# Attention with sink rows and a two-layer MLP on one core: the sink rows' copies, their value tile, and seven numbers of the planner

## The chip, the cores and the metric

One Trainium2 chip, one core. The metric is the device time of one launch in microseconds (us), the median of several runs; three runs of the kernel before are shown.

## The reference

```python
B, H, S, D = 4, 8, 768, 64; n_sink, window = 4, 128
scores = (1 / sqrt(D)) * q @ k.T                       # per batch and head
keep = (key < n_sink) | (0 <= query - key < window)    # 4 sink keys and a band of 128
a = softmax(where(keep, scores, -1e9))
x = (a @ v) laid out as [B * S, H * D]                 # 3072 x 512
h = x @ w_in                                           # 512 -> 2048
out = (h - tanh(h)) @ w_out                            # 2048 -> 512
```

All inputs are float32 (the host hands the weights over as 64-bit words, which the kernel decodes).

## The kernel before

The work is cut into 12 chunks of 256 queries (4 batches of 3 chunks), and a chunk into 4 units, u0 to u47, of one pair of heads each. The first three chunks are the first chunks of batches 0, 1 and 2 (units u0 to u11); their attention stands at the head of the program.

A unit's attention: TensorE (PE) makes two tiles of scores (L487 for the first 12 units, L494 later), VectorE (DVE) merges and masks them (L506, L512), ScalarE (ACT) exponentiates (L520, two instructions and two accumulator reads per tile) and scales (L546, four instructions per unit) with the sums that DVE prepares (L540, L541). PE transposes the probabilities (`turn`, L573), ACT and DVE copy them out of PSUM under the band masks (L580, L587). The columns of the four sink keys go another way: GpSimd (POOL) collects them, high and low parts, in the small tile `z` (L551 to L553).

`attend` (L596 to L657) puts two pairs (first three chunks) or four pairs (the rest) together. `sink_rows` transposes `z` on PE into the upper half of the PSUM tile `x` (L604), `sink_copy` copies it to `zr` on ACT (L611), and `values` multiplies: one matmul of 512 columns for each two pairs with the sink values `vsink` (L621), then the band's values (L627). `x_high` (ACT, L639) and `x_low` (DVE, L643) split the result into two parts of a reduced format (fp32r). `x` has one buffer, so the next `sink_rows` waits for `x_low`. In the kernel before `zr` is made twice, by two instructions with a factor of 0 or 1 per row (`odd`), one for each pair of a bank.

`sink_values(b, due)` (L410 to L437) prepares `vsink` for a batch: SP loads `vraw`, ACT copies it into two blocks of 64 rows (`high`, L420), POOL takes the rest and masks it (`low`, L424, L425), DVE adds both under the mask `half` (`total`, L429). It is called for batches 0, 1, 2 in the first three chunks, and four times more later. `sink_half` (L399) makes the masks.

The MLP runs in 96 steps n0 to n95 (a chunk and one of 8 groups of weights each): `first_half` is 24 matmuls of 256 columns (L699), in quarters of 6, `gate` is tanh, difference, high and low part on ACT and DVE (L704 to L715), `second_half` 12 matmuls of 512 columns (L747). `weights(k, g)` decodes group g of w_in (k=0) or w_out (k=1): three DVE passes (L154 to L158), a high part on ACT (L674), a low part on DVE (L679).

Every engine's queue is written in the order of a planner (`Work`, L167 to L228): each piece has an engine, a guessed duration, a due time and the names that it reads and writes; the planner places, engine by engine, the ready piece that is due first. FIRST, EARLY, UNIT, WLEAD, WNEXT, ZL and SV set due times, SLACK a margin ahead of PE's pieces. What counts on the chip is the order that comes out; real waits are semaphores between the engines.

Of the kernel before, what the change touches and what calls it, by code (L numbers as in the profile page):

```python
# [166 lines left out]
class Work:  # L167
# [5 lines left out]
    WAKE = {"PE": 250, "ACT": 170, "DVE": 90, "POOL": 100, "SP": 80}  # L173
    SLACK = 400

# [55 lines left out]
def _banded(tc, qd, kp, vp, vs, masks, w_in, w_out, ident, pts, early, out):  # L231
    nc = tc.nc
    et = mybir.EngineType
    with ExitStack() as ctx:
# [12 lines left out]

        RAW, TWO, CUT, DUO, PB, ZL, TK = 12, 12, 2, 3, 4, 0, 1100

# [6 lines left out]
        NS = len(order)  # L256
        FIRST, EARLY, PACE, LEAD = 50000.0, 5000.0, 7200.0, 16000.0
        UNIT, SECOND, WLEAD, WNEXT = 2200.0, 0.0, 0.0, 2500.0

# [122 lines left out]
        halfi = cpool.tile([P, 1], I32, tag="halfi", name="halfi")  # L382
        vsink = cpool.tile([P, 2, P], F32R, tag="vsink", name="vsink")
        vraw = cpool.tile([P, P], F32, tag="vraw", name="vraw")

        zt = cpool.tile([P, 2, NPAIR, 4, 2, NSK], F32R, tag="z", name="z")

        zr = cpool.tile([P, 2, CH], F32R, tag="zr", name="zr")
        odd = cpool.tile([P, 2], F32, tag="odd", name="odd")
        oddi = cpool.tile([P, 1], I32, tag="oddi", name="oddi")  # L390

        with tc.manual_schedule(engines={et.DVE, et.Pool}):
            mask, above, below, after, rest = masks
            nc.gpsimd.iota(halfi, pattern=[[0, 1]], base=0, channel_multiplier=1)
            nc.gpsimd.iota(oddi, pattern=[[0, 1]], base=0, channel_multiplier=1)
            nc.gpsimd.memset(zt.bitcast(F32), 0.0)
            nc.gpsimd.memset(vsink.bitcast(F32), 0.0)

        def sink_half():  # L399
            for part, bit, pair in ((halfi, 16, half), (oddi, 32, odd)):  # L400
                nc.vector.tensor_scalar(part, part, bit, None, op0=ALU.bitwise_and)
                nc.vector.tensor_copy(pair[:, 0:1], part)
                nc.vector.tensor_scalar(pair[:, 1:2], pair[:, 0:1], 1.0, None, op0=ALU.is_ge)
                nc.vector.tensor_scalar(pair[:, 0:1], pair[:, 0:1], 1.0, None, op0=ALU.is_lt)

        work.add("DVE", 1300, 4000, sink_half, (), ["half"])
        work.add("DVE", 1000, 500, rest, (), ["mask"])
        count = [0]

        def sink_values(b, due):  # L410
            slot = "vraw"

            def load():
                nc.sync.dma_start(vraw, vs[32 * b : 32 * b + 32].rearrange("r (p c) -> p r c", c=P))

            rows = [(slice(64 * i, 64 * i + 64), i) for i in range(2)]

            def high():
                for r, i in rows:
                    nc.scalar.copy(vsink[r, i, :], vraw[r])  # L420

            def low():
                for r, i in rows:
                    nc.gpsimd.tensor_tensor(vraw[r], vraw[r], vsink[r, i, :].bitcast(F32), op=ALU.subtract)  # L424
                nc.gpsimd.tensor_scalar(vraw, vraw, half[:, 1:2], 1.0, op0=ALU.mult, op1=ALU.mult)  # L425

            def total():
                for r, i in rows:
                    nc.vector.scalar_tensor_tensor(  # L429
                        vsink[r, i, :], vsink[r, i, :].bitcast(F32), half[r, 0:1], vraw[r],  # L430
                        op0=ALU.mult, op1=ALU.add,
                    )
# [163 lines left out]
        def attend(cc, p0, pairs):  # L596
# [456 lines left out]
```

## Time and profile before

| | us |
|---|---|
| median of 3 runs | 693.4 (692.64 to 693.81) |
| the profiled execution | 693.47 |
| its span, first to last instruction | 691.7 |
| PE busy in it | 677.0 (98%) |
| DVE, ACT, POOL busy | 427.4, 367.8, 54.5 |

The profile is of one execution. The span leaves out some 1.8 us around the instructions. A busy PE is not PE at its peak: matmuls overlap, and their ends are modelled, so that the step from one start to the next tells more than a duration.

### The profile page before, as it was taken

What the parts mean: (1) busy time and instruction counts of PE and PEld (TensorE: products, weight loads), DVE (VectorE), ACT (ScalarE), POOL (GpSimd) and SP (SyncE); (2) the same over time, 40 slices, a digit from 0 to 9 for tenths busy, and PEclk for the clock granted to TensorE, in tenths of its full rate; (3) what the DMA queues carried; (4) which work ended last, traced back from release to release, by engine and by line L of the source; (5) the groups of instructions that cost most, each with busy time, mean ns of one, the idle gap of its engine ahead of it and who ended that gap; (6) DMA issues with size and microseconds to landing.
All of it is one profiled execution on the core that took longest, in us unless ns stands there. A gap on an engine that the chain in (4) does not pass through costs nothing.

```text
span 691.7 us, 12427 instructions
## 1 busy us (share of the span) xinstructions
PE 677.0 (98%) x4604; PEld 599.7 (87%) x4604; DVE 427.4 (62%) x1084; ACT 367.8 (53%) x1001; POOL 54.5 (8%) x202
## 2 busy tenths in 40 slices
PE   6989999999999999999999999999999999999996
PEld 5668999999988989889988988998898888998985
DVE  6889999946856556646655665565554755663221
ACT  4996433346754555446545645555555545644222
POOL 6331100000000010000001000001000000000000
PEclk9999999999999999999999999999999999999999
DMA  6879801011231032012113202012112101100001
GB/s 177 266 239 383 320 1 32 0 58 59 57 108 33 28 103 59 28 30 91 51 28 108 54 27 90 28 54 80 37 36 80 55 28 59 58 1 1 31 1 35
DMA packets 31713, 52.14 MB, mean 75 GB/s; under 512 B 3228, under 2 KB 21020, under 8 KB 31644
## 3 DMA queue, kind: packets, MB, share of 16 engines
q1 hardware_dynamic: 31340, 50.93, 23.0%
q8 instruction: 38, 0.62, 0.4%
q10 hardware_dynamic: 304, 0.33, 0.2%
q14 instruction: 31, 0.25, 0.1%
HBM read 44.96 MB, written 6.29 MB: 74 GB/s over the span
## 4 chain that ended last, share of the span: by engine, by line
PE 92%; ACT 4%; DVE 1%; SPq 1%; DMA 1%; issue 0%; DVEq 0%
PE h L699 39%; PE o L747 39%; PE s L494 5%; PE x L627 5%; PE t L573 3%; ACT p L546 1%; ACT p L520 1%; PE x L621 1%; DMA pt<-kp 1%; DMA qk<-kp 0%; DVE pt L587 0%; DVE p L512 0%; ACT pt L580 0%; PE x L604 0%; ACT zr L611 0%
## 5 line engine op out<-in xcount | busy, mean ns | idle before, releaser
L699 PE MATMUL h<-xh,w 128*128 128x256 f32 x1536 | 285.4, 280 | 0.0
L699 PEld LDWEIGHTS h<-xh,w 128*128 128x128 f32 x1536 | 240.3, 188 | 2.2 <-issue 0.5
L699 PE MATMUL h<-xl,w 128*128 128x256 f32 x768 | 214.7, 279 | 0.6 <-DVE xl L643 0.6
L747 PE MATMUL o<-w,gh 128*128 128x512 f32 x768 | 199.5, 400 | 0.0
L747 PEld LDWEIGHTS o<-w,gh 128*128 128x128 f32 x768 | 137.5, 188 | 27.3 <-issue 0.3
L699 PEld LDWEIGHTS h<-xl,w 128*128 128x128 f32 x768 | 144.2, 188 | 2.3 <-DVE xl L643 1.0
L747 PE MATMUL o<-w,gl 128*128 128x512 f32 x384 | 106.1, 397 | 0.0
L520 ACT ACTIVATE p<-p,st 128x132 f32<-128x132 f32 x192 | 76.1, 399 | 53.9 <-DVE st L512 53.0
L715 DVE TENSOR_TENSOR gl<-h,gh 128x512 fp32r<-128x512 f32 x96 | 66.2, 689 | 50.6 <-ACT gh L711 50.4
L704 ACT ACTIVATE graw<-h 128x512 f32<-128x512 f32 x96 | 57.0, 594 | 69.8 <-PE h L699 69.7
L707 DVE TENSOR_TENSOR h<-h,graw 128x512 f32<-128x512 f32 x96 | 66.5, 692 | 44.5 <-ACT graw L704 43.9
L711 ACT CAST gh<-h 128x512 fp32r<-128x512 f32 x96 | 55.6, 579 | 58.7 <-DVE h L707 58.7
L747 PEld LDWEIGHTS o<-w,gl 128*128 128x128 f32 x384 | 71.1, 188 | 17.3 <-issue 1.0
L506 DVE COPY_PREDICATED s<-above,s 128x256 f32<-128x256 uint32 x80 | 34.1, 426 | 83.0 <-PE s L494 80.8
L546 ACT ACTIVATE p<-p,st 128x132 f32<-128x132 f32 x192 | 61.8, 395 | 4.5 <-DVE st L541 4.1
L512 DVE CUSTOM_DVE_ANT_0 p<-s,mask 128x132 f32<-128x132 f32 x192 | 48.9, 293 | 6.5 <-PE s L487 0.2
L551 POOL CAST z<-p 128x16 fp32r<-128x16 f32 x48 | 11.8, 246 | 501.6 <-ACT p L546 492.6
L461 ACT CAST q<-qraw 128x512 fp32r<-128x512 f32 x36 | 22.4, 622 | 53.7 <-PE s L494 50.2
L494 PEld LDWEIGHTS s<-ks,q 128*128 128x128 f32 x288 | 42.8, 188 | 4.8 <-issue 0.2
L494 PE MATMUL s<-ks,q 128*128 128x260 f32 x288 | 46.6, 284 | 0.0
L643 DVE TENSOR_TENSOR xl<-x,xh 128x512 fp32r<-128x512 f32 x24 | 16.5, 690 | 43.8 <-ACT xh L639 43.8
L456 DVE TENSOR_TENSOR ks<-kraw,ks 64x392 fp32r<-64x392 f32 x72 | 40.4, 561 | 3.1 <-ACT ks L451 0.9
(82 smaller groups left out, 574.6 us busy)
## 6 DMA issues: line engine op xcount, KB each, us to landing
qraw<-qd SPq DMA_DIRECT2D x36, 256.0 KB, 2.7
wraw<-w_in SPq DMA_DIRECT2D x16, 512.0 KB, 8.9
wraw<-w_out SPq DMA_DIRECT2D x16, 512.0 KB, 9.3
kraw<-kp SPq DMA_DIRECT2D x37, 196.0 KB, 2.7
v<-vp SPq DMA_DIRECT2D x27, 256.0 KB, 2.9
out<-ob SPq DMA_DIRECT2D x24, 256.0 KB, 2.5
qk<-kp SPq DMA_DIRECT2D x8, 196.0 KB, 4.6
qk<-qd SPq DMA_DIRECT2D x16, 64.0 KB, 4.7
```

What stands on the lines that cost most here:

```text
L456: nc.vector.tensor_tensor(k[o, h, :], t[r, :], k[r, h, :].bitcast(F32), op=ALU.subtract)
L494: nc.tensor.matmul(ps[h][:, :WIN], lhsT=q[:, h, t * P : (t + 1) * P], rhs=rhs, start=i == 0, stop=i == 1,)
L512: nc.vector.tensor_tensor_reduce(out=pr[u][:, j, :], in0=ps[h][:, P:WIN], in1=mask[:, kind, :], scale=-0.125, scalar=BIG, op0=ALU.add, op1 ...
L520: nc.scalar.activation(e, e, AF.Exp, bias=st[u][:, j : j + 1], scale=-1.0, accum_out=st[u][:, 4 + j : 5 + j],)
L546: nc.scalar.activation(pr[u][:, j, :], pr[u][:, j, :], AF.Copy, scale=s[:, 8 + j : 9 + j])
L627: nc.tensor.matmul(xps[key][(p - p0) // 2][h * 64 : h * 64 + 64, p % 2, a:z], lhsT=vt[cc, i][:, hd : hd + D], rhs=rhs, start=False, stop=p ...
L699: nc.tensor.matmul(hps[n][:, f, :], lhsT=w, rhs=x, start=r == 0, stop=r == 11)
L704: nc.scalar.activation(gr[n], hps[n], AF.Tanh)
L707: nc.vector.tensor_tensor(hps[n], hps[n], gr[n], op=ALU.subtract)
L711: nc.scalar.copy(gh[n], hps[n])
L715: nc.vector.tensor_tensor(gl[n], hps[n], gh[n].bitcast(F32), op=ALU.subtract)
L747: nc.tensor.matmul(ops[cc, t], lhsT=(gh, gh, gl)[i][n][:, f, t * P : (t + 1) * P], rhs=wt[1, g][:, (0, 1, 0)[i], f, :], start=first and no ...
```

## The change

The changed kernel copies the transposed sink rows once and unmasked into `zr` (one ACT instruction of 256 columns instead of two). `vsink` becomes a tile with a block of 128 columns for each of the four pairs, zero outside the pair's 32 rows, and `values` multiplies once per pair (256 columns) instead of once per two pairs (512 columns). `high` writes four blocks of 32 rows on ACT with the factor `half` (+1 or -1) from a per-row operand, `total` adds four blocks on DVE; POOL's `low` is gone, and the four instructions of `sink_half` that made `odd`. Seven numbers of the planner move, one (SV) is new, and the guessed durations of `high`, `total`, `sink_copy` and `sink_half` are adapted.

```diff
-    SLACK = 400
+    SLACK = 350
...
-        RAW, TWO, CUT, DUO, PB, ZL, TK = 12, 12, 2, 3, 4, 0, 1100
+        RAW, TWO, CUT, DUO, PB, ZL, TK, SV = 12, 12, 2, 3, 4, 4000, 1100, 14000
...
-        FIRST, EARLY, PACE, LEAD = 50000.0, 5000.0, 7200.0, 16000.0
-        UNIT, SECOND, WLEAD, WNEXT = 2200.0, 0.0, 0.0, 2500.0
+        FIRST, EARLY, PACE, LEAD = 45000.0, 4600.0, 7200.0, 16000.0
+        UNIT, SECOND, WLEAD, WNEXT = 2400.0, 0.0, 6000.0, 3500.0
...
-        vsink = cpool.tile([P, 2, P], F32R, tag="vsink", name="vsink")
+        vsink = cpool.tile([P, NPAIR, P], F32R, tag="vsink", name="vsink")
...
-        zr = cpool.tile([P, 2, CH], F32R, tag="zr", name="zr")
+        zr = cpool.tile([P, CH], F32R, tag="zr", name="zr")
...
         def sink_half():
-            for part, bit, pair in ((halfi, 16, half), (oddi, 32, odd)):
-                nc.vector.tensor_scalar(part, part, bit, None, op0=ALU.bitwise_and)
-                nc.vector.tensor_copy(pair[:, 0:1], part)
-                nc.vector.tensor_scalar(pair[:, 1:2], pair[:, 0:1], 1.0, None, op0=ALU.is_ge)
-                nc.vector.tensor_scalar(pair[:, 0:1], pair[:, 0:1], 1.0, None, op0=ALU.is_lt)
+            nc.vector.tensor_scalar(halfi, halfi, 16, None, op0=ALU.bitwise_and)
+            nc.vector.tensor_copy(half[:, 0:1], halfi)
+            nc.vector.tensor_scalar(half[:, 1:2], half[:, 0:1], 1.0, None, op0=ALU.is_ge)
+            nc.vector.tensor_scalar(half[:, 0:1], half[:, 1:2], -2.0, 1.0, op0=ALU.mult, op1=ALU.add)
...
-            rows = [(slice(64 * i, 64 * i + 64), i) for i in range(2)]
+            rows = [(slice(32 * p, 32 * p + 32), p) for p in range(NPAIR)]
             def high():
-                for r, i in rows:
-                    nc.scalar.copy(vsink[r, i, :], vraw[r])
-            def low():
-                for r, i in rows:
-                    nc.gpsimd.tensor_tensor(vraw[r], vraw[r], vsink[r, i, :].bitcast(F32), op=ALU.subtract)
-                nc.gpsimd.tensor_scalar(vraw, vraw, half[:, 1:2], 1.0, op0=ALU.mult, op1=ALU.mult)
+                for r, p in rows:
+                    nc.scalar.activation(vsink[r, p, :], vraw[r], AF.Copy, scale=half[r, 0:1])
             def total():
-                for r, i in rows:
+                for r, p in rows:
                     nc.vector.scalar_tensor_tensor(
-                        vsink[r, i, :], vsink[r, i, :].bitcast(F32), half[r, 0:1], vraw[r],
-                        op0=ALU.mult, op1=ALU.add,
+                        vsink[r, p, :], vraw[r], half[r, 1:2], vsink[r, p, :].bitcast(F32), op0=ALU.mult, op1=ALU.add,
                     )
...
-            def sink_copy(m):
-                nc.scalar.activation(zr[:, m, :], xps[key][0][:, 1, :], AF.Copy, scale=odd[:, m : m + 1])
+            def sink_copy():
+                nc.scalar.copy(zr, xps[key][0][:, 1, :])
...
-                for i in banks:
-                    nc.tensor.matmul(xps[key][i], lhsT=vsink[:, p0 // 2 + i], rhs=zr, start=True, stop=False)
+                for p in range(p0, p0 + pairs):
+                    nc.tensor.matmul(
+                        xps[key][(p - p0) // 2][:, p % 2], lhsT=vsink[:, p], rhs=zr, start=p % 2 == 0, stop=False,
+                    )
...
-        sink_values(0, 10000)
+        sink_values(0, SV)
```

Three places of the order. The first is PE around the end of the second chunk's attention: `x1_2` is the result of its second half, `h0` and `h1` the first layer of steps n0 and n1, `t8` and `t9` the transposes of units u8 and u9, `x2_0` the `sink_rows` of the third chunk. Before:

```order
L573 MATMUL t7_732<-ident_58,p7_566 128x128 x4
...
L487 MATMUL s11_1_760<-qk10_324 128x260 x2
L573 MATMUL t8_772<-ident_58,p8_623 128x128 x4
L621 MATMUL x1_2_746<-zr_250,vsink_247 128x512
...
L699 MATMUL h0_810<-xh0_514,w0_0_741 128x256
L573 MATMUL t9_835<-ident_58,p9_673 128x128 x4
...
L604 MATMUL x2_0_861<-ident_58,z_249 128x128 x2
L699 MATMUL h1_865<-xh1_717,w0_0_741 128x256
```

In the changed kernel (its lines stand some 10 lower here):

```order
L689 MATMUL h0_732<-xh0_516,w0_0_595 128x256
...
L563 MATMUL t7_742<-ident_58,p7_565 128x128 x4
...
L477 MATMUL s11_1_762<-qk10_321 128x260 x2
L563 MATMUL t8_781<-ident_58,p8_622 128x128 x4
L610 MATMUL x1_2_758<-zr_250,vsink_247 128x256 x2
...
L689 MATMUL h0_732<-xh0_516,w0_0_595 128x256
L689 MATMUL h1_843<-xh1_723,w0_0_595 128x256
...
L563 MATMUL t9_856<-ident_58,p9_671 128x128 x4
L594 MATMUL x2_0_871<-ident_58,z_249 128x128 x2
L689 MATMUL h1_843<-xh1_723,w0_0_595 128x256
```

The first quarter of n0 (six matmuls, of which the first is shown) now stands ahead of u7's transposes, and the other three quarters with the first of n1 ahead of u9's (`t9`); before, two quarters of n0 stood there. The third chunk's `sink_rows` (`x2_0`) now stands ahead of n1's second quarter.

The second place is ACT around `sink_copy` of the second chunk's second half (`zr` from `x1_2`), as far as its `x_high` (`xh1` from `x1_2`); `p9`, `p10`, `p11` are the probabilities of u9 to u11. Before:

```order
L611 ACTIVATE zr_250<-x1_2_746,odd_251 128x256 x2
L520 ACTIVATE p10_737,st10_738<-p10_737,st10_738 128x132 x2
L546 ACTIVATE p9_673<-p9_673,st9_674 128x132 x4
L520 ACTIVATE p10_737,st10_738<-p10_737,st10_738 128x132 x2
L520 ACTIVATE p11_768,st11_769<-p11_768,st11_769 128x132 x2
L420 CAST vsink_247<-vraw_248 64x128 x2
L580 COPY pt_60<-t8_772 128x2x128
L639 CAST xh1_717<-x1_2_746 128x512
```

Changed:

```order
L510 ACTIVATE p10_726,st10_727<-p10_726,st10_727 128x132 x2
...
L510 ACTIVATE p10_726,st10_727<-p10_726,st10_727 128x132 x2
L600 CAST zr_250<-x1_2_758 128x256
L536 ACTIVATE p9_671<-p9_671,st9_672 128x132 x4
L536 ACTIVATE p10_726<-p10_726,st10_727 128x132 x4
L510 ACTIVATE p11_773,st11_774<-p11_773,st11_774 128x132 x2
L417 ACTIVATE vsink_247<-vraw_248,half_245 32x128 x4
L570 COPY pt_60<-t8_781 128x2x128
L630 CAST xh1_723<-x1_2_758 128x512
```

The two tiles of u10's exponents, which stood behind, now stand ahead of the copy, and u10's scaling (`p10`, four instructions) has moved in ahead of `xh1`.

The third place is DVE from u8's masks (`t8`) to u9's (`t9`): `xl1` is `x_low` of the same half chunk, `vsink` the `total` of batch 2. Before:

```order
L587 TENSOR_TENSOR pt_60<-t8_772,below_87 128x2x128
L587 TENSOR_TENSOR pt_60<-t8_772,after_88 128x2x128
L643 TENSOR_TENSOR xl1_718<-x1_2_746,xh1_717 128x512
L429 SCALAR_TENSOR_TENSOR vsink_247<-vsink_247,half_245,vraw_248 64x128 x2
L587 TENSOR_TENSOR pt_60<-t9_835,below_87 128x2x128
```

Changed:

```order
L577 TENSOR_TENSOR pt_60<-t8_781,below_87 128x2x128
L577 TENSOR_TENSOR pt_60<-t8_781,after_88 128x2x128
L158 SCALAR_TENSOR_TENSOR pt_60<-wraw1_0_439,pt_60 128x1024
L421 SCALAR_TENSOR_TENSOR vsink_247<-vraw_248,half_245,vsink_247 32x128 x4
L634 TENSOR_TENSOR xl1_724<-x1_2_758,xh1_723 128x512
L577 TENSOR_TENSOR pt_60<-t9_856,below_87 128x2x128
```

`x_low` stood ahead of `total` and stands behind it now, and `total` has four instructions. A decoding pass of w_out's first group (L158) has moved in ahead of both.

## Rows read from the trace of the kernel before

**Rows 1.** The page's busy times (busy us, share of the span, instructions) and its chain of waits by engine.

```profile
PE 677.0 (98%) x4604; PEld 599.7 (87%) x4604; DVE 427.4 (62%) x1084; ACT 367.8 (53%) x1001; POOL 54.5 (8%) x202
...
PE 92%; ACT 4%; DVE 1%; SPq 1%; DMA 1%; issue 0%; DVEq 0%
```

**Rows 2.** Busy time by stretch: the stretch, its length, then busy us (and instructions) of PE, PE's weight loads, DVE, ACT, POOL, the granted clock, DMA share, GB/s.

```profile
6.00:12.33 6.33, 5.92 (x16) 4.23 (x16) 3.71 (x25) 1.98 (x10) 5.61 (x20) 1.00 0.54 152
12.33:48.30 35.97, 32.61 (x192) 23.45 (x192) 31.57 (x146) 35.66 (x141) 11.18 (x37) 1.00 0.79 249
48.30:64.20 15.90, 15.42 (x119) 12.81 (x117) 13.74 (x27) 12.65 (x39) 4.71 (x12) 1.00 0.98 350
64.20:160.00 95.80, 95.80 (x621) 86.54 (x619) 79.25 (x93) 37.90 (x57) 2.21 (x3) 1.00 0.26 95
160.00:690.00 530.00, 525.67 (x3658) 471.25 (x3656) 296.31 (x783) 278.56 (x757) 27.71 (x117) 1.00 0.17 50
```

**Rows 3.** What PE waited for, over the span: us in total, times, longest.

```profile
PE t L573 <- DVE pt L587: 1.4, 2, 1.1
...
PE h L699 <- DVE xl L643: 0.6, 1, 0.6
```

**Rows 4.** The chain that ended last, in order of time, in the dense part: start us, us, what. x24 are 24 matmuls in L699.

```profile
69.27 2.82 PE h L699 x24
72.10 2.80 PE o L747 x12
...
141.93 2.73 PE h L699 x24
```

**Rows 5.** Groups by line over the span: count | busy us, mean ns of one | idle before.

```profile
L699 PEld LDWEIGHTS h<-xh,w 128*128 128x128 f32 x1536 | 240.3, 188 | 2.2 <-issue 0.5 <-DVE w L679 0.2
...
L424 POOL TENSOR_TENSOR vraw<-vraw,vsink 64x128 f32<-64x128 f32 x14 | 7.3, 521 | 62.9 <-ACT vsink L420 62.3
...
L425 POOL TENSOR_SCALAR vraw<-vraw,half 128x128 f32<-128x128 f32 x7 | 3.4, 485 | 0.7
```

**Rows 6.** ACT's timeline: start us, us of all in the row, line, operation, shapes, count [idle before <- releaser]. L520 exponents (a tile is two of them with their accumulator reads), L546 scaling, L580 masks' copies, L611 sink_copy, L420 high, L639 x_high.

```profile
12.33 0.41 ACT L520 ACTIVATE p<-p,st 128x132 f32<-128x132 f32 x1 [0.80 <-DVE st L512]
...
13.12 1.28 ACT L546 ACTIVATE p<-p,st 128x132 f32<-128x132 f32 x4
14.30 0.39 ACT L520 ACTIVATE p<-p,st 128x132 f32<-128x132 f32 x1
...
21.63 0.35 ACT L580 COPY pt<-t 128x256 f32<-128x256 f32 x1
21.88 0.83 ACT L611 ACTIVATE zr<-x,odd 128x256 fp32r<-128x256 f32 x2
22.61 1.28 ACT L546 ACTIVATE p<-p,st 128x132 f32<-128x132 f32 x4
...
33.31 0.63 ACT L420 CAST vsink<-vraw 64x128 fp32r<-64x128 f32 x2
33.96 0.37 ACT L580 COPY pt<-t 128x256 f32<-128x256 f32 x1
...
45.42 0.84 ACT L611 ACTIVATE zr<-x,odd 128x256 fp32r<-128x256 f32 x2
...
50.56 0.59 ACT L639 CAST xh<-x 128x512 fp32r<-128x512 f32 x1
```

**Rows 7.** DVE's timeline, the same columns. The row at 11.38 is the first of sink_half's second four. L643 x_low, L429 total.

```profile
11.38 0.14 DVE L401 TENSOR_SCALAR oddi<-oddi 128x1 int32<-128x1 int32 x1
...
12.00 0.28 DVE L512 CUSTOM_DVE_ANT_0 p<-s,mask 128x132 f32<-128x132 f32 x1
...
51.19 0.69 DVE L643 TENSOR_TENSOR xl<-x,xh 128x512 fp32r<-128x512 f32 x1 [1.15 <-ACT xh L639]
51.80 0.72 DVE L429 SCALAR_TENSOR_TENSOR vsink<-vsink,half,vraw 64x128 fp32r<-64x128 f32 x2
52.76 0.42 DVE L587 TENSOR_TENSOR pt<-t,below 128x256 f32<-128x256 f32 x1 [0.25 <-ACT pt L580]
```

**Rows 8.** DVE's timeline, later: the low part of w_in's last group.

```profile
135.18 1.23 DVE L679 TENSOR_TENSOR w<-pt,w 128x1024 fp32r<-128x1024 f32 x1
```

**Rows 9.** PE's timeline: L621 the sink values' matmul, L627 the band's, L699 first layer, L573 transposes, L747 second layer.

```profile
46.45 0.47 PE L621 MATMUL x<-zr,vsink 128*128 128x512 f32 x1
46.85 1.52 PE L627 MATMUL x<-pt,v 128*64 128x256 f32 x16
48.30 0.38 PE L699 MATMUL h<-xh,w 128*128 128x256 f32 x1
...
50.72 0.66 PE L573 MATMUL t<-ident,p 128*128 128x128 f32 x4 [0.46 <-ACT pt L580]
...
64.20 2.02 PE L747 MATMUL o<-w,gh 128*128 128x512 f32 x8
```

**Rows 10.** SP's queue: DMA issues, start us, us that the issue held the queue.

```profile
15.37 0.43 SPq L312 DMA_DIRECT2D qk<-kp  x1
19.19 0.59 SPq L414 DMA_DIRECT2D vraw<-vs  x1
19.82 1.14 SPq L321 DMA_DIRECT2D qk<-qd  x2
```

More of the change, by code (lines that the diff above doesn't have):

```diff
@@ L382, in _banded @@
         halfi = cpool.tile([P, 1], I32, tag="halfi", name="halfi")
-        vsink = cpool.tile([P, 2, P], F32R, tag="vsink", name="vsink")
+        vsink = cpool.tile([P, NPAIR, P], F32R, tag="vsink", name="vsink")
         vraw = cpool.tile([P, P], F32, tag="vraw", name="vraw")
         zt = cpool.tile([P, 2, NPAIR, 4, 2, NSK], F32R, tag="z", name="z")
-        zr = cpool.tile([P, 2, CH], F32R, tag="zr", name="zr")
-        odd = cpool.tile([P, 2], F32, tag="odd", name="odd")
-        oddi = cpool.tile([P, 1], I32, tag="oddi", name="oddi")
+        zr = cpool.tile([P, CH], F32R, tag="zr", name="zr")
         with tc.manual_schedule(engines={et.DVE, et.Pool}):
@@ L394, in _banded @@
             nc.gpsimd.iota(halfi, pattern=[[0, 1]], base=0, channel_multiplier=1)
-            nc.gpsimd.iota(oddi, pattern=[[0, 1]], base=0, channel_multiplier=1)
             nc.gpsimd.memset(zt.bitcast(F32), 0.0)
@@ L399, in sink_half @@
         def sink_half():
-            for part, bit, pair in ((halfi, 16, half), (oddi, 32, odd)):
-                nc.vector.tensor_scalar(part, part, bit, None, op0=ALU.bitwise_and)
-                nc.vector.tensor_copy(pair[:, 0:1], part)
-                nc.vector.tensor_scalar(pair[:, 1:2], pair[:, 0:1], 1.0, None, op0=ALU.is_ge)
-                nc.vector.tensor_scalar(pair[:, 0:1], pair[:, 0:1], 1.0, None, op0=ALU.is_lt)
-        work.add("DVE", 1300, 4000, sink_half, (), ["half"])
+            nc.vector.tensor_scalar(halfi, halfi, 16, None, op0=ALU.bitwise_and)
+            nc.vector.tensor_copy(half[:, 0:1], halfi)
+            nc.vector.tensor_scalar(half[:, 1:2], half[:, 0:1], 1.0, None, op0=ALU.is_ge)
+            nc.vector.tensor_scalar(half[:, 0:1], half[:, 1:2], -2.0, 1.0, op0=ALU.mult, op1=ALU.add)
+        work.add("DVE", 650, 4000, sink_half, (), ["half"])
         work.add("DVE", 1000, 500, rest, (), ["mask"])
@@ L414, in load @@
                 nc.sync.dma_start(vraw, vs[32 * b : 32 * b + 32].rearrange("r (p c) -> p r c", c=P))
-            rows = [(slice(64 * i, 64 * i + 64), i) for i in range(2)]
+            rows = [(slice(32 * p, 32 * p + 32), p) for p in range(NPAIR)]
             def high():
-                for r, i in rows:
-                    nc.scalar.copy(vsink[r, i, :], vraw[r])
-            def low():
-                for r, i in rows:
-                    nc.gpsimd.tensor_tensor(vraw[r], vraw[r], vsink[r, i, :].bitcast(F32), op=ALU.subtract)
-                nc.gpsimd.tensor_scalar(vraw, vraw, half[:, 1:2], 1.0, op0=ALU.mult, op1=ALU.mult)
+                for r, p in rows:
+                    nc.scalar.activation(vsink[r, p, :], vraw[r], AF.Copy, scale=half[r, 0:1])
             def total():
-                for r, i in rows:
+                for r, p in rows:
                     nc.vector.scalar_tensor_tensor(
-                        vsink[r, i, :], vsink[r, i, :].bitcast(F32), half[r, 0:1], vraw[r],
-                        op0=ALU.mult, op1=ALU.add,
+                        vsink[r, p, :], vraw[r], half[r, 1:2], vsink[r, p, :].bitcast(F32), op0=ALU.mult, op1=ALU.add,
                     )
             work.add("SP", 400, due - 9000, load, (), [slot], lands=300)
-            work.add("ACT", 500, due - 3500, high, [slot], ["vsink"])
-            work.add("POOL", 1000, due - 3000, low, ["half", "vsink"], [slot], port=True)
-            work.add("DVE", 500, due - 1000, total, [slot], ["vsink"], port=True)
+            work.add("ACT", 1000, due - 3500, high, [slot, "half"], ["vsink"])
+            work.add("DVE", 1000, due - 1000, total, [slot], ["vsink"], port=True)
         qh, ql, ks, pr, st, xps, xh, xl, sps, tps = ({} for _ in range(10))
@@ L647, in attend @@
             work.add("PE", 230, d + 1500, sink_rows, [("z", i) for i in range(NPAIR)], ["x"])
-            for m in range(2):
-                work.add("ACT", 270, d + 2000, lambda m=m: sink_copy(m), ["x"], [("zr", m)])
+            work.add("ACT", 300, d + 2000, sink_copy, ["x"], ["zr"])
             v = [vslot[cc, i] for i in range(max(0, 2 * c - 1), 2 * c + 2)]
             pt = [(f"pt {k}", place(NPAIR * cc + i)) for k in ("whole", "own", "before") for i in range(p0, p0 + pairs)]
-            need = pt + ["vsink", ("zr", 0), ("zr", 1)] + v
+            need = pt + ["vsink", "zr"] + v
             work.add("PE", (340 + 735 * pairs if c == 0 else 200 + TK * pairs), d + 3500, values, need, ["x", "t"][: pairs // 2])
```

## The prediction

> **What bounds the kernel now.** First the page's busy times and the chain's shares [rows 1]: PE is busy for 98% of the span and holds 92% of the chain. A busy share can hide waiting inside overlapping matmuls, so the stretches come next [rows 2]. From 64.20 us PE shows no idle time up to 160 us and some 4 of 530 us after that, and in the chain a step's 24 matmuls of 256 columns take 2.82 us, its 12 of 512 columns 2.80 us, one step behind the other [rows 4]: PE does nothing but the MLP, at 0.1175 us and 0.233 us a matmul, at a granted clock of 1.00 (the 2.4 GHz level). PE's list of waits has a single one of 0.6 us behind the head of the program [rows 3]. Nothing that the change takes from ACT, DVE or POOL there shortens the span.
>
> The head is different. From 12.33 to 48.30 us ACT is busy for 35.66 of 35.97 us, DVE for 31.57 [rows 2]. ACT paces the first three chunks' attention, and PE follows it; from 48.30 us the MLP's first steps fill PE, so that the next 15.90 us hold few gaps. The change is decided by when PE gets past that point, and with how much work done.
>
> I use starts, not durations, for prices, because instructions overlap: an exponent tile holds ACT for 0.79 us (12.33 to 13.12), a unit's scaling for 1.18 us (four instructions), two sink copies for 0.73 us (21.88 to 22.61), the copy of 256 columns out of PSUM for 0.25 us (21.63 to 21.88), the two instructions of `high` for 0.65 us (33.31 to 33.96) [rows 6].
>
> **The edits, each with its price.**
>
> *Start.* DVE stands in `sink_half` when the second unit's first merge is due: its second four instructions begin at 11.38 us, the merge at 12.00 us [rows 7], and ACT waits 0.80 us for that merge [rows 6]. They go: **−0.62 us** at the point from which ACT is never idle. The wait that is next, for PE's scores of that unit, is over by then, since DVE's row at 12.00 us notes no idle time.
>
> *Sink copy.* Two instructions become one without a factor. Its nearest row is the other 256-column copy from PSUM, 0.25 us; half of the pair, 0.37 us, is the dear end. That saves 0.48 us (at least 0.36) in each of the six attends of the head: **−2.9 us** of ACT (−2.2).
>
> *High.* Two copies become four with a per-row factor, 128 columns each. The row nearest in kind is the scaling, 132 columns with a per-row factor: 1.18 us for four, so +0.53 us. The dear end is 0.40 us each, if instructions on different rows don't overlap, as the two of `high` don't (0.65 us for two of 0.30): 1.6 us, +0.95. Batches 0 to 2 lie in the head: **+1.6 us** (+2.85). The four later ones lie beside a dense PE.
>
> *Total.* Two products took 0.72 us [rows 7]; four take 1.44 us, +0.72 on DVE, in a queue that is 88% busy in the head. Its place counts, below.
>
> *POOL.* The 21 instructions of `low` (7.3 and 3.4 us [rows 5]) go. They lay beside ACT and DVE; POOL has 54.5 us in all [rows 1]. Nothing.
>
> *PE.* Each bank's 512-column matmul becomes two of 256: 0.235 us for 0.233, nothing over 24 banks, given that the 24 added weight loads hide. Each load lasts 188 ns [rows 5], and yet load and matmul together step at 0.1175 us in the stream [rows 4].
>
> *SP.* The load for batch 1's sink rows waited for its buffer and held the queue from about 17 to 19.19 us, u6's queries behind it [rows 10]. It now stands behind u7's queries too. No PE wait in the head is for a load of those units, so nothing.
>
> *Decoding later.* Weights come out of DVE in another order up to about 145 us. The last w_in group is ready at 136.4 us [rows 8] and first used at 141.93 us [rows 4]; the change's 1 to 2 us more of DVE work leave that margin of 5.5 us open. Nothing; without it, the loss would be what exceeds the margin.
>
> **The sum, at PE's turning point.** ACT's sink copy of the second chunk's second half starts at 45.42 us [rows 6], and PE's matmul on it at 46.45 us [rows 9]. In the new order two more exponent tiles stand ahead of it (+1.58), two batches of `high` are dearer (+1.06), three earlier copies are cheaper (−1.44), and the start is earlier (−0.62): +0.58. The copy itself is 0.48 us shorter, so PE gets its operand **0.1 us later**. But it already has the first quarter of step n0 behind it, six matmuls: **−0.71 us**.
>
> Then the stretch from 48.30 to 64.20 us, 15.90 us. Its work is nine quarters of first layer (6.35), twelve second-layer matmuls (2.80), three transposes (1.3), two `sink_rows` (0.45) and two `values` at 1.85 us (46.45 to 48.30): 14.6 us. So 1.3 us are lost, 1.0 of it at once: twelve matmuls, 1.41 us of work, take from 48.30 to 50.72 us, the last 0.46 us waiting for ACT [rows 9]. That loss goes, since weights are decoded earlier and four quarters stand there now. A new one comes: `x_high` was at 50.56 us [rows 6]; ahead of it now stand u10's scaling (+1.18), three dearer `high` (+1.6), four cheaper copies (−1.9), less the start (−0.62): 50.8 us. `high` ends just before that, and DVE has a decoding pass and four products (1.44 us) to do ahead of `x_low` (0.6 us), which used to stand first. `x_low` ends near 52.9 us, and `sink_rows`, in front of n1's second quarter on PE, waits for it until 53.0 us. PE is there at 48.4 + 2.8 + 0.45 = 51.7 us. **Loss 1.3 us instead of 1.0: +0.3.**
>
> Sum: +0.1 − 0.7 + 0.3 = −0.3 us, against the profiled execution's 693.47 us: 693.2 us. That execution lies 0.07 us above the median of 693.4, so I forecast **693.1 us**: what ACT gains, the reordering and the new wait on DVE eat up. A measurement of this kernel can tell 0.2%, 1.4 us, from no change; this is inside.
>
> **Rivals.**
>
> *PE keeps all that ACT gains.* ACT is the bottleneck of the head [rows 2], and its balance to the end of the third chunk is −0.62 − 2.9 + 1.6 = −1.9 us. If `x_low` isn't late (DVE runs ahead and `high` comes early), PE ends that much sooner: 691.6 us. For it speaks ACT's 99% from 12.33 us; against it, that PE, not ACT, runs dense from 48.30 us, and DVE's 88%. Chance 0.30.
>
> *The four products hold up `x_low`.* If the instructions of `high` don't overlap (0.40 us each) and the copy costs 0.37 us, PE's operand comes 1.4 us later (1.58 + 1.9 − 1.1 − 0.62 − 0.36), and `x_high` 1.9 us later, at 52.5; `x_low` ends at 54.3, and PE, there at 53.0, waits until 54.4. That makes 1.4 − 0.7 + 0.4 = +1.1. DVE meets the same wait in front of unit 5's second merge, where four products stand behind ACT's first `high`; bounded by 1.44 us, half of it is +0.7. Together 695.2 us. It decides from 1.4 us a batch for `high` upwards. The pair of 0.65 us speaks for it, the earlier decoded weights (more to fill PE with) against. Chance 0.13.
>
> *The added weight loads show.* 24 loads at 188 ns are 4.5 us: 697.9 us. The stream at 0.1175 us per pair speaks against it. The Trainium skill has a rule by which they would show: in "TensorE: Matmul & The Clock Gate", "The mechanism", a weight load overlaps running matmuls only if their row groups differ, and all of these use 128 rows; with its price in "LDWEIGHTS (loading the stationary operand)", columns divided by 1.2, in ns, an estimate is 24 × 107 ns = 2.6 us. By that rule the sum would be 695.7 us; the trace disagrees, with load and matmul of 128 rows in 0.1175 us, less than the 188 ns of the load alone. Chance 0.03.
>
> That the change does not do what it says has a small form: POOL keeps collecting sink columns, so it isn't idle, and the time stays at 693.4 us. That lies in the forecast's case.
>
> **How the numbers follow.** Forecast's case 0.54, first rival 0.30, second 0.13, third 0.03: faster by over 0.2% 0.30, within 0.54, slower 0.16. The range goes from the first rival, 691.6, less 0.4 for a part of the 1.0 us lost at 48.30 us, to just short of the second, with half of its bound at unit 5 gone: 691.2 to 694.9 us. The forecast's own case is 692.1 to 694.5.
>
> **What would show it.** Right: the second unit's first exponent near 11.7 us; a sink copy of 0.25 to 0.37 us; `high` at 1.2 us for four; a wait of PE at the third chunk's `sink_rows`, ended by `x_low` near 53 us; PE's second-layer matmuls of n1 (64.20 us) within 1 us of that; the dense part as it was, with a matmul per pair at 0.1175 us. Wrong: PE at that point before 63 us, or after 65.5 us, or new gaps behind 70 us.

## The result

The changed kernel takes **697.51 us** (median), the kernel before 693.4 us: ratio **1.0061, 95% interval 1.0049 to 1.0073**. It is slower by 0.6%, outside the range that was forecast (691.2 to 694.9 us). One of the five executions took 831.83 us, at a granted clock of 0.75, and the ratio is taken without it. The profiled execution's span is 695.7 us, 4.0 us longer than before.

The page's busy times and the chain's shares, as [rows 1]:

```profile
PE 677.9 (97%) x4628; PEld 603.8 (87%) x4628; DVE 430.7 (62%) x1094; ACT 368.9 (53%) x1000; POOL 44.2 (6%) x180
...
PE 90%; ACT 5%; DVE 2%; issue 1%; DMA 1%; SPq 0%; ACTq 0%
```

Busy sums don't show the loss: PE has 0.9 us more, ACT 1.1 us more, POOL 10 us less. Nor do the stretches, the columns those of [rows 2]:

```profile
12.33:48.30 35.97, 30.82 (x186) 23.61 (x185) 30.86 (x142) 35.46 (x140) 8.19 (x30) 1.00 0.82 259
48.30:64.20 15.90, 14.61 (x115) 12.27 (x113) 14.31 (x31) 12.36 (x36) 4.21 (x9) 1.00 0.91 324
160.00:690.00 530.00, 528.49 (x3688) 475.46 (x3686) 298.53 (x790) 277.58 (x755) 22.98 (x108) 1.00 0.17 49
```

Behind 160 us PE looks busier than before (528.49 us for 525.67), though some two microseconds are lost there. What shows them is the same instruction's start in both timelines. The difference, after less before, is +1.57 us at n1's second layer (before 64.20 us [rows 9], now the row at 65.77 us below), about +1.6 at 195 us and +1.9 from 252 to 365 us; +2.95 at 380 us; +3.0 up to 475 us; +4.0 at 487 us; +3.8 at 681 us. So **1.6 us are lost in the head and 1.0 us at each of two later places**. The rest, +0.25 us near 200 to 250 us and -0.2 us near 635 us, stands in kernels with a short `high` as well.

The head, on DVE and ACT (answering to [rows 6, 7]; L502 merges, L510 exponents, L600 the sink copy, L417 `high`, L536 scaling, L570 mask copy, L630 `x_high`, L421 `total`, L634 `x_low`):

```profile
11.45 0.30 DVE L502 CUSTOM_DVE_ANT_0 p<-s,mask 128x132 f32<-128x132 f32 x1
...
52.13 1.47 DVE L421 SCALAR_TENSOR_TENSOR vsink<-vraw,half,vsink 32x128 fp32r<-32x128 f32 x4
53.62 0.69 DVE L634 TENSOR_TENSOR xl<-x,xh 128x512 fp32r<-128x512 f32 x1
```

```profile
11.79 0.41 ACT L510 ACTIVATE p<-p,st 128x132 f32<-128x132 f32 x1 [0.38 <-DVE st L502]
...
20.77 0.35 ACT L600 CAST zr<-x 128x256 fp32r<-128x256 f32 x1
21.02 1.66 ACT L417 ACTIVATE vsink<-vraw,half 32x128 fp32r<-32x128 f32 x4
22.71 0.41 ACT L536 ACTIVATE p<-p,st 128x132 f32<-128x132 f32 x1
...
50.89 1.66 ACT L417 ACTIVATE vsink<-vraw,half 32x128 fp32r<-32x128 f32 x4
52.57 0.37 ACT L570 COPY pt<-t 128x256 f32<-128x256 f32 x1
52.84 0.59 ACT L630 CAST xh<-x 128x512 fp32r<-128x512 f32 x1
```

The start is 0.54 us earlier (11.79 us for 12.33). The sink copy takes 0.25 us from start to start. The four writes of `high` take **1.69 us** (21.02 to 22.71), where two took 0.65: 0.42 us each, none starting before the one ahead has ended. `total` takes 1.47 us, and `x_low` stands behind it. PE (L610 the sink values' matmuls, L594 `sink_rows`, L737 second layer), as [rows 9]:

```profile
48.11 0.48 PE L610 MATMUL x<-zr,vsink 128*128 128x256 f32 x2
48.52 1.52 PE L618 MATMUL x<-pt,v 128*64 128x256 f32 x16
...
54.46 0.41 PE L594 MATMUL x<-ident,z 128*128 128x128 f32 x2 [0.81 <-DVE xl L634]
...
65.77 2.13 PE L737 MATMUL o<-w,gh 128*128 128x512 f32 x8
```

The two matmuls take 0.41 us, as the one of 512 columns did (0.40): the added weight loads cost nothing. But they start 1.66 us later than at 46.45 us.

The later places are seen in the chain that ended last. Before, between 366 and 375 us (48 first-layer matmuls, a transpose of scaled scores, the second layer, of which the view, cut at 375 us, has eight matmuls):

```profile
366.89 5.66 PE h L699 x48
372.55 0.44 PE t L573 x4
372.99 2.04 PE o L747 x8
```

After, the same place:

```profile
369.44 0.28 ACT vsink L417
...
371.01 0.62 ACT q L451
...
374.01 0.76 ACT p L536 x3
...
375.31 0.48 ACT gh L701
...
375.82 3.06 PE o L737 x12
```

Before, the chain stays on PE. After, it leaves PE for ACT: `high`, a query split, exponents, scaling, and then `gh`, on which the second layer waits until 375.82 us, 2.8 us later than 372.99; the work ahead of that place was 1.9 us later. Near 486 us it is the same. These are the first units of the third and the fourth batch, where ACT's queue holds that batch's `high`.

### The profile page after: what moved, and what is told of

It reads as the page before. It is cut to its first block, busy times and chain, and to the rows that moved or that the text cites. A ratio compares the mean times of both kernels' runs of the same rounds, so it can differ in the third digit from the quotient of the medians.

```text
span 695.7 us, 12455 instructions
## 1 busy us (share of the span) xinstructions
PE 677.9 (97%) x4628; PEld 603.8 (87%) x4628; DVE 430.7 (62%) x1094; ACT 368.9 (53%) x1000; POOL 44.2 (6%) x180
## 4 chain that ended last, share of the span: by engine, by line
PE 90%; ACT 5%; DVE 2%; issue 1%; DMA 1%; SPq 0%; ACTq 0%
PE o L737 39%; PE h L689 37%; PE x L618 5%; PE s L484 5%; PE t L563 2%; ACT p L536 2%; PE s L477 1%; ACT p L510 1%; ACT vsink L417 1%; PE x L610 1%; DMA pt<-qd 1%; DVE p L502 1%; DVE pt L577 0%; ACT pt L570 0%; PE x L594 0%
## 5 line engine op out<-in xcount | busy, mean ns | idle before, releaser
L737 PE MATMUL o<-w,gh 128*128 128x512 f32 x768 | 199.5, 400 | 0.3
L737 PEld LDWEIGHTS o<-w,gh 128*128 128x128 f32 x768 | 138.0, 188 | 28.5 <-ACT gh L701 1.1
L510 ACT ACTIVATE p<-p,st 128x132 f32<-128x132 f32 x192 | 76.1, 398 | 61.0 <-DVE st L502 60.2
L737 PE MATMUL o<-w,gl 128*128 128x512 f32 x384 | 106.3, 397 | 0.0
L737 PEld LDWEIGHTS o<-w,gl 128*128 128x128 f32 x384 | 71.0, 188 | 17.1 <-issue 1.0
L536 ACT ACTIVATE p<-p,st 128x132 f32<-128x132 f32 x192 | 61.7, 395 | 4.9 <-DVE st L531 4.2
L502 DVE CUSTOM_DVE_ANT_0 p<-s,mask 128x132 f32<-128x132 f32 x192 | 48.9, 292 | 7.0 <-PE s L477 0.3
L541 POOL CAST z<-p 128x16 fp32r<-128x16 f32 x48 | 10.1, 211 | 579.7 <-ACT p L536 561.7
L634 DVE TENSOR_TENSOR xl<-x,xh 128x512 fp32r<-128x512 f32 x24 | 16.5, 690 | 42.1 <-ACT xh L630 42.1
```

Source lines behind the costliest of these rows:

```text
L502: nc.vector.tensor_tensor_reduce(out=pr[u][:, j, :], in0=ps[h][:, P:WIN], in1=mask[:, kind, :], scale=-0.125, scalar=BIG, op0=ALU.add, op1 ...
L510: nc.scalar.activation(e, e, AF.Exp, bias=st[u][:, j : j + 1], scale=-1.0, accum_out=st[u][:, 4 + j : 5 + j],)
L536: nc.scalar.activation(pr[u][:, j, :], pr[u][:, j, :], AF.Copy, scale=s[:, 8 + j : 9 + j])
L737: nc.tensor.matmul(ops[cc, t], lhsT=(gh, gh, gl)[i][n][:, f, t * P : (t + 1) * P], rhs=wt[1, g][:, (0, 1, 0)[i], f, :], start=first and no ...
```

## The experiments

Theory A: the loss is ACT's time in `high`. B: it is the planner's new numbers and the order that they make. C: PE's added matmuls and weight loads. Each ratio is to runs of the kernel before that were made beside the run (their medians lie between 693.0 and 693.6 us), so kernels of different experiments are compared by their ratios. The diffs show the lines that matter; `...` stands for others. "The head" below is the start of n1's second layer (before 64.20 us, after 65.77 us).

**One instruction for `high`**, then the same in the four later batches alone (`vm` lies in a tile that is free at that moment; the order on PE, ACT and DVE is that of the changed kernel):

```diff
-                for r, p in rows:
-                    nc.scalar.activation(vsink[r, p, :], vraw[r], AF.Copy, scale=half[r, 0:1])
+                nc.scalar.activation(vm, vraw, AF.Copy, scale=half[:, 0:1])
...
-                        vsink[r, p, :], vraw[r], half[r, 1:2], vsink[r, p, :].bitcast(F32), ...
+                        vsink[r, p, :], vraw[r], half[r, 1:2], vm[r].bitcast(F32), ...
```

> The changed kernel with `high` as one ACT instruction over 128 partitions into a temporary tile, which `total` then reads; the order on every engine, the planner's numbers, the one sink copy and the PE split matmuls stay as changed. Theory A (the loss is ACT's time in `high`, 1.66 us for four writes where two took 0.65 us): each `high` falls to about 0.30 us. In the steady part ACT reaches the pieces that PE's transposes and second-layer matmuls wait for 1.3 us earlier, so the two jumps of 1.0 us at the batch changes (transposes at 374.5 and 485.9 us) vanish, -2.05 us; the head gets back between nothing and its whole 1.6 us. 693.9 to 695.5 us. Theory B (the planner's new numbers and the order they make): nothing of that order changes here, so 697.0 to 698.0. Theory C (PE's 24 added matmuls and weight loads): unchanged too, 697.0 to 698.0.

> The same, but only the four later batches' `high` is one instruction; the three of the head keep their four writes. Theory A: the second-layer matmuls of n1 start at 65.8 us as in the changed kernel, and the two jumps at 374 and 486 us vanish: 697.5 - 2.05 = 695.4 us. Theories B and C: 697.0 to 698.0. The difference to the run with all seven short is what the head's three writes cost.

Measured: all seven short **692.12 us, ratio to before 0.9985 (0.9976 to 0.9994)**; only the later four short 694.69 us, 1.0024 (1.0014 to 1.0034). The first is below its range, which gave the head back 1.6 us at most; the second is 0.7 us below the 695.4 us expected. ACT and PE of the first (L420 `high`, L457 the query split; L743 second layer):

```profile
366.45 0.41 ACT L420 ACTIVATE zr<-vraw,half 128x128 fp32r<-128x128 f32 x1
366.75 0.62 ACT L457 CAST q<-qraw 128x512 fp32r<-128x512 f32 x1
```

```profile
62.91 2.13 PE L743 MATMUL o<-w,gh 128*128 128x512 f32 x8
```

and its chain at the batch change, on PE again:

```profile
365.92 5.65 PE h L695 x48
...
372.01 2.80 PE o L743 x12
```

`high` takes 0.30 us, both jumps are gone, and the head is 2.86 us earlier than after. With the head's three left long, the head stays (65.43 us; three traces with the same pieces in the head, this one among them, have 65.77, 65.57 and 65.43, so 0.3 us there is no difference), and the jumps go. A holds. C falls: all 24 matmuls are in the kernel that beats both others.

**The planner's numbers crossed**: the changed code with the old numbers, and the code before with the new ones. The guessed durations stay with their code.

```diff
-    SLACK = 350
+    SLACK = 400
...
-  ... ZL, TK, SV = ... 4000, 1100, 14000;  FIRST, EARLY = 45000.0, 4600.0;  UNIT, ... WLEAD, WNEXT = 2400.0, ... 6000.0, 3500.0
+  ... ZL, TK, SV = ... 0, 1100, 10000;     FIRST, EARLY = 50000.0, 5000.0;  UNIT, ... WLEAD, WNEXT = 2200.0, ... 0.0, 2500.0
```

> The changed kernel's instructions with the planner's constants of the kernel before (SLACK 400, ZL 0, FIRST 50000, EARLY 5000, UNIT 2200, WLEAD 0, WNEXT 2500, first sink values due at 10000). Theory A: four writes of `high` stay at 1.66 us, so both steady jumps stay (+2.05 us against before) and the head is at best as before: 695.5 us or more. Theory B: with the old numbers the time goes back to 693.4, within 0.7 us.

> The kernel before with the planner's constants of the changed one, its instructions as they were (two `high` of 64 rows, POOL's part, two masked sink copies). Theory A: no jumps at the batch changes behind 200 us, the head alone may move, by up to 2 us either way: 691.5 to 695.5 us, with the steady part from 70 us on as long as before within 0.5 us. Theory B: slower by most of the 4.1 us, 696 to 698 us.

Measured: 698.30 us, 1.0073 (1.0059 to 1.0086), and 700.03 us, 1.0093 (1.0078 to 1.0109). With the old numbers the changed code keeps both jumps (+1.0 us each) and loses 2.6 us in the head: the old numbers are no cure, and B as the cause falls. But A's range for the second kernel (to 695.5) was missed by 4.5 us. Its steady part has no jumps, as A says; all 6 us are lost by 78 us, with n2's second layer. PE there, and by stretch (columns as in [rows 2]):

```profile
29.69 0.41 PE L604 MATMUL x<-ident,z 128*128 128x128 f32 x2
32.57 1.09 PE L573 MATMUL t<-ident,p 128*128 128x128 f32 x4 [2.47 <-DVE pt L587]
...
34.02 2.83 PE L627 MATMUL x<-pt,v 128*64 128x256 f32 x16
```

```profile
32.00:36.00 4.00, 3.43 (x17) 2.45 (x19) 3.93 (x16) 4.00 (x16) 0.01 (x1) 0.50 0.95 320
36.00:40.00 4.00, 4.00 (x19) 3.05 (x18) 1.48 (x9) 2.18 (x9) 1.27 (x3) 0.69 0.58 187
```

In that order PE waits 2.47 us for DVE, and by the end of the wait the granted clock has fallen to 0.50 (the 1.2 GHz level): the 16 band matmuls take 2.83 us instead of 1.52 [rows 9]. From the two stretches, half of 4 us and 0.31 of 4 us, 3.2 us of PE's pace are gone at most. Neither the numbers nor the code alone came out better than the two together; for the changed code the difference (1.0073 for 1.0061) lies inside the intervals, for the code before the new numbers cost 0.9%.

**The planner told the true durations**, in the kernel with the single `high`:

```diff
-            work.add("ACT", 1000, due - 3500, high, ...)
-            work.add("DVE", 1000, due - 1000, total, ...)
+            work.add("ACT", 300, due - 3500, high, ...)
+            work.add("DVE", 1470, due - 1000, total, ...)
```

> The kernel with the single `high` (692.1 us), and the planner told what its two sink steps take, 300 ns for `high` and 1470 ns for `total`, where it held 1000 and 1000. The durations stay, the order in the head is another. Theory A (the time of the instructions decides, the order by little): 691.4 to 692.8 us. Theory B (the order that the planner's numbers make is a term as large as the durations): over 1 us from 692.1 us, either way.

Measured: 696.80 us, 1.0042 (1.0028 to 1.0055), 0.6% above the single `high` with the wrong guesses. A's expectation missed. In the traced execution, one of the shorter (695.02 us), waits of PE for DVE (2.2 us for the masks' products, 1.5 us for `x_low`, 0.8 us for the sums) and ACT (0.7 us for `gh`) put it 2.7 us later at n2's second layer (73.35 us for 70.69); where the other 1.8 us of the median lie was not traced. So the order is a term as large as the durations; in the change as made, it is not the one that cost.

**The place of `high`.** The changed kernel, with the later `high` and `total` of the third and the fourth batch ten steps lower in ACT's order, in an idle gap:

```diff
+        for n, m in list(zip(steps("ACT", "sink_values.<locals>.high"), steps("DVE", "sink_values.<locals>.total")))[-2:]:
+            act = [k for k in todo if work.all[k][0] == "ACT"]
+            to = act[act.index(n) + 10]
+            todo.remove(n)
+            todo.remove(m)
+            i = todo.index(to) + 1
+            todo[i:i] = [n, m]
```

> The changed kernel, its `high` still four writes of 1.66 us, but in the two last batches `high` and `total` are moved 10 steps down ACT's order, to where ACT stood idle for 2.0 us (behind the exponent at 380.5 us and its like near 492 us); nothing else moves. Theory A (it is where `high` stands that makes it cost: ACT's pieces for PE were just in time there): both jumps of 1.0 us vanish though not one instruction is cheaper: 697.5 - 2.05 = 695.4 us, 694.7 to 695.8. Rival (the 1.0 us a batch follows the work, ACT or DVE being full in the steady part): 697.0 to 698.0 us.

Measured: **695.03 us**, 1.0026 (1.0016 to 1.0036), where theory A had 694.7 to 695.8. The chain at the place of the first jump, and ACT behind it:

```profile
368.64 5.65 PE h L689 x48
374.30 0.44 PE t L563 x4
374.73 2.80 PE o L737 x12
```

```profile
379.76 1.65 ACT L417 ACTIVATE vsink<-vraw,half 32x128 fp32r<-32x128 f32 x4
```

No instruction is cheaper, and both jumps are gone. It was not the work but where it stood: ahead of ACT pieces that PE took the moment they were ready. `total` moved along, but it is not the cause: in the kernel with the single `high` it stands where it stood, and the jumps are gone there too.

**The forecast's own price for `high`**: four copies of 128 rows.

```diff
+                    for i in (1, 0, 1, 0):
+                        nc.scalar.activation(t[:, i * P : (i + 1) * P], vraw, AF.Copy, scale=half[:, 0:1])
```

> The kernel with the single `high`, now four scaled copies of 128 rows, in turn into two halves of a temporary tile: the price that the forecast gave `high`, 4 x 0.295 = 1.18 us; near 84 us two scaled copies of 64 rows instead. Theory A: two jumps of 1.18 - 0.65 = 0.5 us against before at the transposes near 371 and 482 us, +1.0 us where the forecast had nothing, and the head 1.4 to 2.0 us later than with the single `high`: 694.3 to 695.2 us. Were the forecast's cover there at its own price: no jumps, 693.3 to 694.0 us. If copies of 128 rows do not overlap each other here either (0.42 us each), `high` is 1.7 us and the time that of the changed kernel, 697.0 to 698.0 us.

Measured: **694.15 us**, 1.0016 (1.0007 to 1.0025), just below theory A's range. ACT, and PE at n1's second layer:

```profile
367.31 1.28 ACT L425 ACTIVATE zr<-vraw,half 128x128 fp32r<-128x128 f32 x4
368.49 0.61 ACT L462 CAST q<-qraw 128x512 fp32r<-128x512 f32 x1
```

```profile
63.77 2.13 PE L748 MATMUL o<-w,gh 128*128 128x512 f32 x8
```

At 1.18 us (367.31 to 368.49) the price is exactly the forecast's, the head is 0.43 us earlier than before (the forecast's sum was -0.3) and 0.9 us later than with the single `high` (theory A's 1.4 to 2.0 us were too much), and both places still jump, by 0.5 us each. So two things failed apart from each other: the cover (+1.0 us even at the forecast's price) and the price (the other 3 us).

**Prices of the forms of `high`** (the diff: other forms in later batches).

> The kernel with the single `high`, where three later batches take other forms, for their prices: four scaled copies of 128 rows near 84 us, four 32-row copies without the scale near 255 us (that batch's low parts come out unsplit), four scaled 32-row copies near 369 us, the single one near 480 us. If it is the short rows that keep ACT from starting the next instruction early: 4 x 0.29 = 1.2 us, then four times the 0.31 us that a 64-row copy took before, 1.2 to 1.3 us or more, then 1.66 us. If it is the scale read from SBUF that costs: 1.66, 1.2, 1.66 us. Theory A has one jump of 1.0 us behind 100 us, at the transposes near 371 us, where the four short scaled copies stand; none near 482 us.

A single execution, 693.03 us. ACT's rows near 80, 254 and 366 us:

```profile
79.62 1.71 ACT L424 ACTIVATE zr<-vraw,half 128x128 fp32r<-128x128 f32 x4
...
253.79 1.26 ACT L427 CAST zr<-vraw 32x128 fp32r<-32x128 f32 x4
...
366.49 1.66 ACT L430 ACTIVATE zr<-vraw,half 32x128 fp32r<-32x128 f32 x4
```

and the two scaled copies of 64 rows near 80 us in the kernel of the preceding experiment:

```profile
80.48 0.81 ACT L422 ACTIVATE zr<-vraw,half 64x128 fp32r<-64x128 f32 x2
```

Unscaled, 32 rows take 0.32 us each from start to start, as 64 rows did before; scaled 0.42. Scaled 64 rows take 0.41, scaled 128 rows 0.295 if the next goes elsewhere, but 0.43 if all four write the same place, which was not expected. So a scale read from SBUF adds 0.1 us, and 128-row instructions to different places overlap by 0.1 us where the short ones don't. The Trainium skill, "ScalarE: Activation LUTs", "What ACT_TABLE_LOAD costs", gives both numbers, measured on tiles of 128 rows: about 93 ns for a pointer operand, and 93 ns of overlap between neighbours. The first agrees; the second holds here for 128 rows to different places, and not for 32 or 64 rows. The place near 366 us jumped by 1.0 us, and the one with the single copy (near 482 us) did not.

**Sink copy twice**, in the kernel with the single `high` and in the changed one:

```diff
-                nc.scalar.copy(zr, xps[key][0][:, 1, :])
+                for _ in range(2):
+                    nc.scalar.copy(zr, xps[key][0][:, 1, :])
```

> The kernel with the single `high` (692.1 us), its unmasked sink copy written twice over, so that ACT holds as many copies as before the change; nothing else moves. Theory A (ACT paces the head, and what it saves or spends there shows): each copy in the head adds the 0.25 to 0.37 us that one takes, and the second-layer matmuls of n1 start 1.3 to 2.2 us after the 62.9 us of the single `high`; behind 70 us it is nothing: 693.4 to 694.3 us. Rival (the copies wait for PE's sink rows in any case, so one or two make no difference): within 0.5 us of 692.1 us, 62.9 us in the head unmoved.

> The changed kernel, `high` in four writes as it is, with its sink copy written twice over. With the single `high` the second copy cost the head 0.3 us for five copies; ACT is 4 us more loaded here. If ACT paces this head, each of five copies adds 0.25 to 0.37 us to it: 698.7 to 699.4 us, the second-layer matmuls of n1 at 67 us or later. If the copies stand where ACT waits for PE's sink rows in any case: 697.3 to 698.1 us.

Measured: 692.68 us, 0.9986 (0.9977 to 0.9995), and 698.42 us, 1.0080 (1.0063 to 1.0096). ACT in the first (L542 scaling):

```profile
45.24 0.76 ACT L607 CAST zr<-x 128x256 fp32r<-128x256 f32 x2
45.90 2.47 ACT L542 ACTIVATE p<-p,st 128x132 f32<-128x132 f32 x8
```

A pair takes 0.66 us for 0.25: six of them hold ACT 2.4 us longer. In the first kernel the head is 0.3 us later (63.21 us), no more than heads with the same pieces differ, and the ratio is that of the single `high` (0.9986 for 0.9985): there the rival's case holds. In the second the head is 0.8 us later (66.54 us), the time lies between the two theories' ranges, and the intervals overlap (1.0080 for 1.0061). That 0.8 us cannot be read as a price of the copies either, since the granted clock fell in that execution:

```profile
31.00:34.00 3.00, 3.00 (x17) 2.34 (x18) 2.62 (x13) 3.00 (x13) 0.92 (x3) 0.50 0.82 282
```

Until then the second copies had cost PE nothing (the scores behind the second `sink_rows` start at 30.08 us, in the changed kernel at 30.07). So what ACT spends at the copies was not seen to reach PE.

**`x_low` ahead of `total`** on DVE, in the kernel with the single `high`:

```diff
+        for n, m in zip(dve, dve[1:]):
+            f, g = work.all[n][3], work.all[m][3]
+            if f.__name__ == "total" and "x_low" in g.__code__.co_freevars:
+                todo.remove(n)
+                todo.insert(todo.index(m) + 1, n)
```

> The kernel with the single `high` (692.1 us), and on DVE alone `x_low` put ahead of `total` at the two places in the head where it stood right behind it; no other instruction moves. Theory D (PE's two waits for `x_low` ahead of the sink rows, 0.9 us each at 37.6 and 52.1 us, are lost time): the waits go, n1's second layer is 0.9 to 1.8 us earlier than 62.9 us, 690.3 to 691.2 us. Rival (behind each wait PE waits next for DVE's merge or ACT's pieces, which do not come earlier): within 0.5 us of 692.1 us.

Measured: 691.92 us, 0.9979 (0.9969 to 0.9990), beside 0.9985 for the other order: no difference that can be told. In the traced execution (692.78 us) n1's second layer is at 63.38 us, no earlier than 62.91. PE's waits in the head of the kernel with `total` first, then with `x_low` first:

```profile
PE x L600 <- DVE xl L640: 1.8, 2, 0.9
```

```profile
PE t L569 <- DVE pt L583: 1.7, 2, 1.1
PE t L569 <- DVE st L536: 1.3, 1, 1.3
```

The waits for `x_low` go, and PE waits instead for the products and sums that `total` now holds up. Theory D falls.

## Why the prediction was wrong, point by point

- *Start*, -0.62 us: right (-0.54).
- *Sink copy*, 0.48 us less each: the price was right (0.25 us for a copy), its worth was not. Doubling the copies again, +2.4 us on ACT, was not seen to reach PE with the single `high`; so the -2.9 us that the first rival counts in full were not worth that.
- *High*: the first of two steps that failed, a term that was mis-sized, +1.04 us a batch for the forecast's +0.53. The forecast took the 128-row scaling (four in 1.18 us) as the nearest row and kept 1.6 us as the dear end; it was 1.69 us. The row of two 64-row copies that didn't overlap, which the forecast names, was the nearer one: it shares what decides, fewer than 128 rows. The dear end needed the larger chance.
- *The sum at PE's turning point* was right but for that price. With `high` at the forecast's own 1.18 us its four times come out: `values` at 46.64 us (forecast 46.45 + 0.1), `x_high` at 50.83 (50.8), `x_low` done at 52.84 (52.9), `sink_rows` at 52.99 (53.0). PE and ACT of that kernel (L621 `values`, L605 `sink_rows`, L641 `x_high`):

```profile
46.64 0.48 PE L621 MATMUL x<-zr,vsink 128*128 128x256 f32 x2
...
52.99 0.41 PE L605 MATMUL x<-ident,z 128*128 128x128 f32 x2 [0.95 <-DVE xl L645]
```

```profile
50.83 0.57 ACT L641 CAST xh<-x 128x512 fp32r<-128x512 f32 x1
```

One link of it is luck as far as is known: the forecast has PE wait for the sink copy's operand, but `values` follows PE's own transposes without a gap, in this kernel as before and after.
- *"The four later ones lie beside a dense PE"*: the second step that failed. It was read from the share of PE (100% busy) that nothing on ACT matters there. But a dense PE takes ACT's `gh` the moment it is there. ACT and PE of the kernel before, at the first of the two places (L711 `gh`, L747 second layer):

```profile
372.28 0.56 ACT L711 CAST gh<-h 128x512 fp32r<-128x512 f32 x1
```

```profile
372.89 2.13 PE L747 MATMUL o<-w,gh 128*128 128x512 f32 x8
```

`gh` ends at 372.84 us, and the second layer goes on at 372.89: the cover was 0.05 us thick. At the second place it was 0.04 us (483.14 and 483.18). What ACT spends more ahead of it shows in full: +1.0 us twice in the change, +0.5 us twice at the forecast's own price. The first two of the four later ones, near 82 and 255 us, cost nothing. The forecast never read ACT's timeline at the batch changes. Either failure alone would have left the time near the end of the forecast's range, 694.9 us: 694.15 us with the forecast's price, 694.69 and 695.03 us without the jumps.
- *Total*, +0.72 us: right (1.47 us for four).
- *POOL, SP, decoding later*, nothing: no wait of PE in the steady part came from them. At w_in's last group the offset is the head's +1.6 us, no more.
- *PE's matmuls*, nothing: right.
- *The operand of the second chunk's second half*, +0.1 us: +1.66. *`sink_rows` waits 1.3 us for `x_low`*: 0.81 us, at 54.46 us instead of 53.0; by the swap on DVE it is no loss of its own.
- *The second rival* is what the head did. For a `high` that doesn't overlap it had the operand 1.4 us later, `x_high` at 52.5 us and PE waiting until 54.4; the trace has 1.66, 52.84 and 54.46. Its time, 695.2 us, and the two jumps, 2.05 us, make 697.25; measured were 697.51. It had named 1.4 us a batch as the point from which it decides: at 1.18 us the head is 63.77 us, at 1.69 us 65.77. Not all of its terms agree: it had the sink copy at 0.37 us (0.25), and its 0.7 us at unit 5's merge were not measured by themselves, so the closeness of the sum is in part luck. From 0.30 to 1.18 us three `high` hold ACT 2.6 us more and PE 0.86; from there 1.5 us more cost PE 2.0; why more than ACT's own time stays open (the two kernels' `high` also write different tiles). The rival had a chance of 0.13. No rival held the jumps behind 70 us.
- *The first rival* (PE keeps what ACT gains, 691.6 us) is near the single `high`, 692.12 us, by luck: there ACT has some 4.6 us less to do in the head (an estimate: 0.62 + 2.9 by the forecast's prices, and 3 x 0.35 for `high`), and PE is 1.29 us earlier.

Of the loss, the head's +1.57 and the jumps' +2.05 us are shown to hang on `high`. Not tried: why the new order was good for the changed code and bad for the one before, instruction by instruction.

## What to carry to other kernels

That an engine is dense says that it loses nothing now, not that its suppliers have time to spare: before an edit on a supplier counts as covered, read at each place where it will stand how long its next piece lies ready before the dense engine takes it. Take an unknown instruction's price from the row that shares its partitions and operands, not its width alone; and if one instruction over all rows can do it, use a spare tile for it: that made the slower kernel the faster one. Where a planner makes the order, correcting a duration in it moves everything: time that as an edit of its own.

## What was not expected of the hardware

Scaled ACT copies of 128 columns: 0.295 us each for 128 rows to different places, 0.43 us to the same place, 0.41 us for 64 rows and 0.42 us for 32; unscaled ones of 32 and 64 rows 0.32 us. Why short ones don't overlap stays open. In the kernel before with the new numbers PE's wait of 2.47 us was followed by a granted clock of 0.50 and 0.69 over the next two stretches of 4 us. In the changed kernel with doubled copies it was 0.50 from 31 to 34 us, behind waits of 1.50 us (to 28.32) and 0.76 us (to 30.08). The changed kernel itself waits 1.19 and 0.76 us at the same two places and 1.56 us at 40.53, and its granted clock stays at 1.00 there.
